# Products of taps ordered between the scatters of GpSimd in a fused convolution and mixture-of-experts kernel

## The chip, the cores and the metric

The kernel runs on one core of a Trainium2 chip. The metric is the device time of one execution in microseconds (us); the time of a kernel is the median of its runs. The engines are named as the profile names them: PE (TensorE), DVE (VectorE), ACT (ScalarE), POOL (GpSimd) and SP (SyncE, whose queue issues most of the transfers).

## The reference

A causal convolution of 7 taps, whose weights come per token and head from a softmax, is followed by a mixture of 8 experts, of which each token uses one.

```python
# x (8, 3584, 192) f32, weight_gen (8, 3584, 8, 7) f32
w = softmax(weight_gen, axis=-1)
out = np.einsum('bshk,bskhg->bshg', w, x_unf)      # x_unf: 7 tokens up to this one, 8 heads of 24
x = out.reshape(28672, 192)
logits = x @ w_gate                                 # 192 x 8
e_idx = np.argmax(logits, axis=1)
gate_w = softmax(logits)[e_idx]
eom = 1.0 / (1.0 + np.exp(-(x @ w_output_gate)))
for e in range(8):
    h = np.maximum(x[e_idx == e] @ w1[e], 0.0)      # 192 x 1024
    out[e_idx == e] = gate_w * eom[:, e] * (h @ w2[e])   # 1024 x 192
```

## The kernel before

The work has two halves that run side by side. The first half, called the front here, goes over 32 units of 896 tokens (u = 0 to 31, 7 tokens in each of 128 partitions). The second half goes over 81 tiles of up to 512 rows, all of one expert.

A unit passes these steps. Its x and its weights are loaded (`load_steps`). `softmax_steps` makes the weights. `tap_steps` makes one product x times weight for each tap: from unit 7 on, GpSimd makes taps 0 to 4 (tiles `gap`, each by two instructions, since the tokens before the unit lie in another buffer) and VectorE taps 5 and 6, and VectorE adds all seven in PSUM (`acc_steps`, rows `ps<-ps,gap`). For units 0 to 6 GpSimd makes four taps and TensorE adds them. There are five buffers for GpSimd's products from unit 7 on and one accumulator. `sum_steps` scales the sum and writes it in two halves of 16-bit numbers to the row buffer `rt`, of which there are three (RT); the rows are transposed by DMA (`gt`), TensorE multiplies them by the gate weights (rows `ps<-gm,gt`, the logits), and VectorE finds each token's expert. `weight_of_steps` computes the token's factor. `place_steps` computes each token's row in a buffer sorted by experts in DRAM, and then GpSimd sends the rows there by seven indirect DMAs, one for each token of a partition (`srtd<-rt,posi`). These are the first kind of scatter. `round_steps` finds out, after each unit, which tiles of 512 rows are certainly full; rows for which no full tile is certain stay back until the last unit.

A tile is loaded by the SP queue (`tile_load`: its rows transposed to `xT`, the expert's weights `wa` and `wb`), behind the scatters of its rows. TensorE multiplies it (`gemm_steps`): for a tile of 512 rows 40 matmuls with `wa`, whose results ScalarE and VectorE split into two halves (`hh`, `hl`), and for each group of 128 rows 24 matmuls with `wb`. ScalarE scales a group into `ys` (two buffers of four groups), and GpSimd sends it to the tokens' rows of the output by one indirect DMA (`out_dram<-ys,meta`). This is the second kind of scatter. The first six tiles (DEFER) are kept in DRAM and sent at the end (`out_dram<-yk,keep`).

The order of all engines' instructions is fixed when the program is made, by a list scheduler in the kernel itself. Every chain of steps is a generator that yields the engine of its next step. `Order.step` takes, again and again, the chain with the smallest key: the planned time at which its step could begin, which is the latest of the scheduler's clock, the chain's own time and the engine's time `t`; between equal times the chain of the smaller rank. Ranks, from first to last, are: split of h, output groups (RANK_Y), placing of rows (RANK_C), rounds, sums (RANK_B), taps (RANK_A), tiles. `Paced` wraps an engine and adds up planned costs to its `t`: a scatter 1.04, a product 0.06 + 0.00174 for each element. So on GpSimd an output group that is ready goes before rows of a unit, and these before a product. Each engine runs its queue in order, and semaphores hold an instruction until its operands are there. The lines of the profile are those of the wrappers: L151 is every compute instruction, L125 every transfer of the SP queue.

Of the kernel before, what the change touches and what calls it, by code (L numbers as in the profile page):

```python
# [67 lines left out]
class Chain:  # L68


    def __init__(self, gen, rank, t, engine):
        self.gen, self.rank, self.t, self.engine, self.gate = gen, rank, t, engine, None
        self.slack = EAGER[1] if len(rank) > 1 and rank[0] in EAGER[2] and rank[1] < EAGER[0] else SLACK
# [33 lines left out]
class Queue:  # L107
# [6 lines left out]
    @property  # L114
    def t(self):
        if self.host is not None:
            return self.host.t
        return max(self.moved, self.issued + self.lead)

    def __getattr__(self, name):  # L120
        f = getattr(self.engine, name)

        def call(*args, **kwargs):
            c, own, issue = self.order.cur, self.cost(name, args, kwargs), self.issue(name, args, kwargs)
            r = f(*args, **kwargs)  # L125
            if self.host is not None:
                self.issued = max(self.host.t, c.t)
                self.host.t = self.issued + issue
            self.issued = max(self.issued, self.order.now) + issue
            if own is not None:  # L130
                self.moved = max(self.moved, self.issued + 0.65) + own
                c.t = max(c.t, self.moved + 1.0)
            return r

        return call


class Paced:


    def __init__(self, order, engine, cost, before=0.0, after=None, lead=0.0, follows=True):
        self.order, self.engine, self.cost, self.t = order, engine, cost, 0.0
        self.before, self.after = before, LAT if after is None else after
        self.lead, self.follows = lead, follows

    def __getattr__(self, name):
        f = getattr(self.engine, name)

        def call(*args, **kwargs):
            c, own = self.order.cur, self.cost(name, args, kwargs)  # L150
            r = f(*args, **kwargs)  # L151
            if own is not None:
                self.t = max(self.t, (c.t if self.follows else self.order.now) + self.before) + own
                c.t = max(c.t, self.t + self.after)
            return r

        return call


def largest(args, kwargs):  # L160
# [50 lines left out]
def kernel(ctx: ExitStack, tc: tile.TileContext, x, wg, wgate, wogate, w1, w2, cst, out):  # L211
# [2 lines left out]
    V = Paced(od, nc.vector, vector_cost)  # L214
    S = Paced(od, nc.scalar, scalar_cost, after=LAT_S)
    G = Paced(od, nc.gpsimd, gpsimd_cost)
    T_ = Paced(od, nc.tensor, tensor_cost, after=0.0)
    SP = Queue(od, nc.sync, sync_cost, sync_issue, LEAD)
    TQ = SP if TURN_SP else Queue(od, nc.scalar, sync_cost, sync_issue, LEAD, S)
# [30 lines left out]
    def take(slots, engine):  # L250

        yield engine, lambda: slots
        got = slots.pop(0)
        od.cur.t = max(od.cur.t, got[0] if isinstance(got, tuple) else got)
        yield engine
        return got
# [27 lines left out]
    def has(u, *what):  # L284
        return lambda: all(k in U[u] for k in what)
# [33 lines left out]
    for i in range(RT):  # L319
        t = rp.tile([P, JS, WR], I32, name=f"rt_{i}")  # L320
# [68 lines left out]
    def gate_steps():  # L389
# [9 lines left out]
        S.activation(gsq, g32.rearrange("p a b -> p (a b)"), AF.Square, accum_out=gss)  # L399
        yield T_  # L400
        pg = ps[:, 2304:2320]
        T_.matmul(pg[:, 0:1], lhsT=ones32, rhs=gss, start=True, stop=True)
        yield V
# [27 lines left out]
    def split_steps(e, st1, st2):  # L431
# [4 lines left out]
        S.activation(sqd, st2, AF.Square, accum_out=ss[:, 1:2])  # L436
        yield from take(tr_free, T_)
        pg = ps[:, 1536:1538]
        T_.matmul(pg[:, 0:2], lhsT=ones32, rhs=ss, start=True, stop=True)
        yield V  # L440
# [101 lines left out]
    def tap_steps(eng, tag):  # L542

        for u in range(NU):
# [12 lines left out]
            while taps:  # L557
# [13 lines left out]
                if u < PE_U:  # L571
                    od.add(add_steps(u, t, tag, kind), (RANK_A, u, 3), T_)
                else:
# [53 lines left out]
    def add_steps(u, t, tag, kind):  # L627

        d = U[u]
        yield T_, lambda: "sum" in d or ("begun" not in d and (u == 0 or "sum" in U[u - 1]))  # L630
        if "begun" not in d:
            d["begun"] = 0
            _, at = yield from take(sum_free, T_)
            d["sum"], d["sum_at"] = ps[:, at : at + 1536], at
        n, flat = d["begun"], t.rearrange("p a b -> p (a b)")
        d["begun"] += 1
        for lo in (0, 512, 1024):
            hi = min(lo + 512, NV * GD)
            T_.matmul(d["sum"][:, lo:hi], lhsT=cf[:, 0:128], rhs=flat[:, lo:hi], start=(n == 0), stop=(n == K - 1 - PAIRS), skip_group_check=True)
        tap_free[tag].append((od.cur.t + LAT_P, kind))  # L640
        if n == K - 1 - PAIRS:
            d["total"] = d["sum"][:, 0 : NV * GD].rearrange("p (a b) -> p a b", b=GD)
            od.add(sum_steps(u), (RANK_B, u), S, T_.t + LAT_P)

    def sum_steps(u):
# [36 lines left out]
        else:  # L682
            od.cur.t += LAT_T
            for j0 in range(0, JS, 2):
# [38 lines left out]
        V.tensor_tensor_scan(out=p3e.rearrange("p e j -> p (e j)"), data0=segs, data1=ohe.rearrange("p e j -> p (e j)"), initial=0.0, op0=ALU.mult, op1=ALU.add)  # L723
        od.cur.t += LAT_R
        yield T_
# [75 lines left out]
    def place_steps(u):  # L801

        d = U[u]
        p3, rk = d["p3"], d["rk"]
        oh1 = d["oh"]
        yield V, has(u - 1, "ranked")
        ob = state["base"]
        ru = f_ru
        V.tensor_tensor(out=ru, in0=rk[:, 0:8], in1=ob, op=ALU.add)
        nb = cp.tile([P, NE], F32, tag="base", bufs=4, name=f"base{u + 1}")  # L810
        V.tensor_tensor(out=nb, in0=rk[:, 8:16], in1=ob, op=ALU.add)
        state["base"] = d["base"] = nb
        rk_free.append((od.cur.t, d["rk_at"]))
        d["ranked"] = True
        if u in plan:
            od.add(round_steps(u), (RANK_R, u), V)
        else:
            state["rounds"] += 1
        yield V
        pe = sp.tile([P, JS, 8], F32, tag="pe", name=f"pe{u}")  # L820
        V.tensor_tensor(out=pe, in0=p3, in1=ru.unsqueeze(1).broadcast_to([P, JS, 8]), op=ALU.add)
        yield V
        V.tensor_tensor(out=pe, in0=pe, in1=oh1, op=ALU.mult)
        done_with(u)
        yield V
        pos = sp.tile([P, JS], F32, tag="pos", name=f"pos{u}")
        V.tensor_reduce(out=pos, in_=pe, axis=AX, op=ALU.add)
        yield S
        posi = sp.tile([P, JS], I32, tag="posi", name=f"posi{u}")
        S.copy(posi, pos)  # L830
        d["placed"] = True
        yield G, has(u, "weighed")
        od.cur.t = max(od.cur.t, d["weighed_t"])
        for j in range(JS):
            yield G
            scattered(G.indirect_dma_start(
                out=srtd[:, :], out_offset=bass.IndirectOffsetOnAxis(ap=posi[:, j : j + 1], axis=0),
                in_=d["ri"][:, j, 0:W], in_offset=None, bounds_check=DUMMY - 1, oob_is_err=False))
        d["sent"] = True
        d["sent_t"] = od.cur.t + 2.5  # L840
        rt_free.append((d["sent_t"], d["ri"]))
# [94 lines left out]
    def tile_load(t, T, ti, i, writers, ka, kb):  # L936
# [11 lines left out]
        SP.dma_start(out=wb, in_=wd[bass.ds(e, 1), :, 2048:WW].rearrange("a p c -> p (a c)"))  # L948
        return dict(t=t, T=T, G=Gn, units=8 // (512 // T), wa=wa.bitcast(F16), wb=wb.bitcast(F16), inv=wb.bitcast(F32)[:, 1536:1537], meta=meta, xT=xT, ka=ka, kb=kb, hh=[], hl=[], hl_t=0.0)

# [22 lines left out]
    def gemm2_group(d, g, at):  # L973
# [6 lines left out]
        for f in range(8):  # L980
# [7 lines left out]
            T_.matmul(py, lhsT=hl, rhs=w2h, start=False, stop=(f == 7))  # L988
        if g == d["G"] - 1:
            wb_free.append((T_.t + WBX, d["kb"]))  # L990
        od.add(out_steps(d, g, py, at), (RANK_Y,), S, T_.t + LAT_P)

    def out_steps(d, g, py, at):
        if g == 0:
            S.activation(d["sc"][:, 0 : d["G"]], d["meta"].bitcast(F32)[:, 0 : d["G"], 0], AF.Copy, scale=d["inv"])
        S.activation(d["ys"][:, g, :], py, AF.Copy, scale=d["sc"][:, g : g + 1])
        y_free.append((od.cur.t, at))
        if d["t"] >= DEFER:
            yield G
            send(d["meta"][:, g, 1:2], d["ys"][:, g, :])  # L1000
        elif g == d["G"] - 1:
            t, n = d["t"], d["G"]
            keep = cp.tile([P, 4], I32, name=f"keep{t}")
            S.copy(keep[:, 0:n], d["meta"][:, 0:n, 1])
            yield SP
            yd = dp.tile([P, n, D], F32, name=f"yd{t}")
            SP.dma_start(out=yd, in_=d["ys"][:, 0:n, :])
            kept.append((keep, yd, n))
# [132 lines left out]
LAT_S = 0.13  # L1141
LAT_P = 0.3
LAT_T = 2.5
LAT_R = 1.0
SLACK = 0.1
EAGER = 0, 0.2, (2, 3, 4)
# [49 lines left out]
```

## Time and profile before

| what | us |
|---|---|
| median of three runs | 1300.61 |
| lowest and highest | 1295.26, 1304.66 |
| profiled execution | 1304.16 |
| its span, first to last instruction | 1302.4 |

The profile is of one execution. In its rows an instruction is named by its line, engine, operation and what it writes and reads (out<-in, the buffers' numbers left out); behind a bar stand the busy time, the mean length of one in ns, and the idle time of the engine just before the instructions, with what ended it. "issue" is idle time that ended for no reason that the profile shows.

### The profile page before, as it was taken

How to read it: one execution, taken by the hardware profiler on the slowest of the kernel's cores; microseconds unless marked ns; L12 is line 12 of the kernel's file. 1: busy time of each engine (PE TensorE's matmuls, PEld its weight loads, DVE VectorE, ACT ScalarE, POOL GpSimd, SP SyncE). 2: the span in 40 equal slices, each digit the busy share in tenths (PEclk: the TensorE clock that was granted, in tenths of full speed). 3: DMA queues.
4: the chain of work that ended last, by engine and by line, in shares of the span. 5: the costliest groups of instructions: out<-in, count | busy, mean ns of one | idle time of the engine just before them, and what ended most of it. 6: DMA issues, size and time to landing. Idle time of an engine off the chain costs nothing.

```text
span 1302.4 us, 28065 instructions
## 1 busy us (share of the span) xinstructions
PE 1147.5 (88%) x9958; PEld 834.1 (64%) x9958; DVE 1021.3 (78%) x2103; ACT 601.8 (46%) x1305; POOL 895.0 (69%) x776
## 2 busy tenths in 40 slices
PE   5886947898697988999997999989899999979998
PEld 2443426676464766676665766666566779878998
DVE  8898866999999999999999999999998633323332
ACT  3674642454353544554454554445454443434443
POOL 7689666667878887888898878998878534322222
PEclk9999878999898999999998999999999999999999
DMA  7777579889777977978797897768867899999994
GB/s 237 228 242 225 175 239 246 226 227 249 201 215 214 241 203 202 272 213 216 205 258 163 262 249 236 202 203 237 211 165 201 220 295 305 320 283 327 308 341 137
DMA packets 293853, 306.18 MB, mean 235 GB/s; under 512 B 232278, under 2 KB 253639, under 8 KB 283344
## 3 DMA queue, kind: packets, MB, share of 16 engines
q1 hardware_dynamic: 271728, 259.78, 70.7%
q0 software_dynamic: 21840, 44.30, 10.6%
q8 instruction: 78, 1.28, 0.4%
q14 instruction: 63, 0.52, 0.1%
q10 hardware_dynamic: 144, 0.31, 0.1%
HBM read 196.42 MB, written 62.01 MB: 198 GB/s over the span
## 4 chain that ended last, share of the span: by engine, by line
PE 38%; DVE 27%; POOL 10%; issue 10%; DMA 9%; ACT 3%; SPq 2%; POOLq 0%; DVEq 0%; ACTq 0%
PE ps L151 38%; DVE ps L151 13%; POOL gap L151 6%; DVE hl L151 4%; POOL srtd L151 3%; SPq L125 2%; DMA w<-in_wg_dram 2%; DVE vap L151 2%; DVE rt L151 2%; DMA wa<-wd 2%; POOL out_dram L151 2%; DMA srtd<-rt,posi 1%; ACT rt L151 1%; DVE w L151 1%; DVE vt L151 1%
## 5 line engine op out<-in xcount | busy, mean ns | idle before, releaser
L151 PE MATMUL ps<-xT,wa 128*128 128x512 f16 (+3 forms) x3240 | 561.1, 324 | 67.0 <-DVE hl L151 30.7
L151 PE MATMUL ps<-wb,hh 128*128 128x192 f16 x3696 | 479.6, 247 | 17.3 <-ACT ys L151 10.5
L151 DVE SCALAR_TENSOR_TENSOR hl<-ps,hh 128x512 f16<-128x512 f32 (+1 forms) x476 | 310.9, 666 | 191.4 <-ACT hh L151 188.3
L151 PE MATMUL ps<-wb,hl 128*128 128x192 f16 x1848 | 456.4, 247 | 0.0
L151 PEld LDWEIGHTS <-wa 128*128 128x128 f16 x3240 | 279.7, 99 | 259.3 <-issue 51.2
L151 POOL TENSOR_TENSOR gap<-x,w 128x960 f32<-128x960 f32 (+5 forms) x268 | 372.4, 1414 | 36.0 <-DVE w L151 13.3
L151 ACT ACTIVATE hh<-ps 128x512 f16<-128x512 f32 (+1 forms) x476 | 274.9, 583 | 229.3 <-PE ps L151 228.5
L151 PEld LDWEIGHTS <-hh 128*128 128x128 f16 x3696 | 337.7, 98 | 65.8 <-issue 25.1
L151 POOL DMA_INDIRECT out_dram<-ys,meta x216 | 214.3, 992 | 235.2 <-ACT ys L151 161.9
L151 POOL DMA_INDIRECT srtd<-rt,posi x224 | 230.0, 1027 | 90.7 <-issue 57.9
L151 ACT ACTIVATE ys<-ps,sc 128x192 f32<-128x192 f32 x231 | 97.1, 421 | 236.1 <-PE ps L151 153.5
L151 DVE TENSOR_TENSOR ps<-ps,gap 128x1344 f32<-128x1344 f32 x125 | 194.1, 1553 | 7.3 <-POOL gap L151 6.4
L151 PEld LDWEIGHTS <-hl 128*128 128x128 f16 x1848 | 181.7, 98 | 0.2
L151 POOL TENSOR_TENSOR gap<-halo,w 128x1152 f32<-128x1152 f32 (+4 forms) x38 | 62.4, 1642 | 18.9 <-issue 13.1
L151 PE MATMUL ps<-gap,cf 128*128 128x512 f32 x168 | 71.9, 566 | 2.7 <-POOL gap L151 2.7
L151 PE MATMUL ps<-vap,cf 128*128 128x512 f32 (+1 forms) x126 | 57.0, 596 | 13.1 <-DVE vap L151 13.1
L151 DVE SCALAR_TENSOR_TENSOR rt<-ps,sx,rt 128x448 f16<-128x448 f32 x64 | 57.6, 907 | 8.4 <-ACT rt L151 4.9
L151 PE MATMUL ps<-gm,gt 128*128 128x32 f16 x672 | 28.1, 177 | 41.0 <-ACT ys L151 12.3
L151 PEld LDWEIGHTS <-gt 128*128 128x128 f16 x672 | 25.2, 96 | 50.9 <-issue 35.7
L151 ACT ACTIVATE rt<-ps 128x1344 bf16<-128x1344 f32 x32 | 41.3, 1291 | 25.4 <-DVE ps L151 20.7
L151 PEld LDWEIGHTS ps<-gap,cf 128*128 128x128 f32 x168 | 31.3, 196 | 32.6 <-issue 26.8
L151 PEld LDWEIGHTS ps<-vap,cf 128*128 128x128 f32 x126 | 24.8, 208 | 36.8 <-issue 23.1
(115 smaller groups left out, 868.7 us busy)
## 6 DMA issues: line engine op xcount, KB each, us to landing
wa<-wd SPq DMA_DIRECT2D x81, 1024.0 KB
wb<-wd SPq DMA_DIRECT2D x81, 768.5 KB
x<-in_x_dram SPq DMA_DIRECT2D x32, 672.0 KB
w<-in_wg_dram SPq DMA_DIRECT2D x32, 196.0 KB
wd<-wpb SPq DMA_DIRECT2D x8, 768.5 KB
st<-in_w_dram SPq DMA_DIRECT2D x8, 768.0 KB
st<-in_w_dram SPq DMA_DIRECT2D x8, 512.0 KB
wd<-wpa SPq DMA_DIRECT2D x8, 512.0 KB
```

The costliest lines, as they stand in the source:

```text
L125: r = f(*args, **kwargs)
L151: r = f(*args, **kwargs)
```

## The change

A class `Apart` stands in for GpSimd where a chain yields it before a scatter. It shows the scheduler GpSimd's planned time plus 0.3 us (APART) when the last thing that GpSimd was given is a scatter, and the plain time otherwise. A product that is ready by then has the smaller key and is taken first, whatever its rank. The scatters themselves, their number and their operands stay as they are, and so do the products. It is used at three yields: two in `place_steps` and one in `out_steps`. The scatters of the six tiles kept back (`kept_steps`) use GpSimd itself.

```diff
@@ class Paced
-        self.lead, self.follows = lead, follows
+        self.lead, self.follows, self.last = lead, follows, None
...
             r = f(*args, **kwargs)
+            self.last = name
...
+class Apart:
+    def __init__(self, engine, name, cost):
+        self.engine, self.name, self.cost, self.lead = engine, name, cost, engine.lead
+
+    @property
+    def t(self):
+        return self.engine.t + (self.cost if self.engine.last == self.name else 0.0)
...
+    GS = Apart(G, "indirect_dma_start", APART)
@@ place_steps
-        yield G, has(u, "weighed")
+        yield GS, has(u, "weighed")
         od.cur.t = max(od.cur.t, d["weighed_t"])
         for j in range(JS):
-            yield G
+            yield GS
             scattered(G.indirect_dma_start(
@@ out_steps
         if d["t"] >= DEFER:
-            yield G
+            yield GS
             send(d["meta"][:, g, 1:2], d["ys"][:, g, :])
...
+APART = 0.3
```

## The prediction

> **What bounds the kernel now.** I read the page's busy line first, then a table of stretches, then the waits of the middle stretch, and last the chain of work that ended last.
>
> The first view is the page's head and its busy times.
>
> ```profile
> span 1302.4 us, 28065 instructions
> PE 1147.5 (88%) x9958; PEld 834.1 (64%) x9958; DVE 1021.3 (78%) x2103; ACT 601.8 (46%) x1305; POOL 895.0 (69%) x776
> ```
>
> TensorE is the busiest engine over the span, but the shares are averages over different stages. The table of stretches separates them: after the first column come the length, then the busy time of PE, PEld, DVE, ACT and POOL with instruction counts, the granted clock, the DMA share and GB/s.
>
> ```profile
> 0.00:300.00 300.00, 229.52 (x1380) 143.56 (x1381) 250.31 (x488) 150.48 (x297) 205.41 (x160) 0.92 0.77 227
> 300.00:1010.00 710.00, 637.99 (x5462) 449.18 (x5460) 670.02 (x1416) 337.59 (x767) 597.84 (x524) 0.98 0.81 219
> 1022.00:1302.00 280.00, 268.52 (x3006) 232.62 (x3003) 96.86 (x195) 109.04 (x232) 86.68 (x89) 0.99 0.90 289
> ```
>
> There are three stages. Up to 300 us the first units and the weights are prepared. From 300 to about 1020 the units of attention (the front) run beside the tiles of the experts: VectorE is busy 670.02 of 710 us (94%), TensorE 90%, GpSimd 84%. From 1022 on only expert tiles are left, and TensorE works 268.52 of 280 us (96%). The chain of work that ended last, in order of time, agrees; its columns are start, length and what:
>
> ```profile
> 1006.06 14.86 PE ps L151 x138
> 1021.42 133.63 PE ps L151 x1399
> 1155.67 6.42 DMA wa<-wd
> 1162.14 2.42 PE ps L151 x40
> 1165.21 5.24 DMA wa<-wd
> 1170.51 123.40 PE ps L151 x1448
> ```
>
> From 1021 on it is TensorE's own work but for two loads of weights. So two things set the time: when the front ends, and how much tile work is then still to do.
>
> GpSimd is fuller than its 84% says. The same stretch, grouped by form on GpSimd, gives its scatters; the columns behind the bar are busy time, mean ns of one, idle time before them and what ended it. Two groups' rows:
>
> ```profile
> L151 POOL DMA_INDIRECT srtd<-rt,posi x160 | 156.9, 980 | 50.7 <-issue 43.3 <-ACT rt L151 3.1 <-DVE w L151 1.6
> L151 POOL DMA_INDIRECT out_dram<-ys,meta x144 | 143.9, 1000 | 58.6 <-issue 17.2 <-ACT ys L151 12.2 <-ACT rt L151 5.4
> ```
>
> There are 160 + 144 = 304 scatters of about 1 us, and nearly all of GpSimd's idle time stands before them. The timeline of GpSimd shows how much of that is no wait at all:
>
> ```profile
> 452.81 2.72 POOL L151 TENSOR_TENSOR gap<-x,w 128x1152 f32<-128x1152 f32 x2
> 455.70 1.01 POOL L151 DMA_INDIRECT out_dram<-ys,meta  x1 [0.17 <-issue]
> 457.02 0.98 POOL L151 DMA_INDIRECT srtd<-rt,posi  x1 [0.30 <-issue]
> 458.30 0.98 POOL L151 DMA_INDIRECT out_dram<-ys,meta  x1 [0.30 <-ACT rt L151]
> 459.58 0.98 POOL L151 DMA_INDIRECT srtd<-rt,posi  x1 [0.30 <-issue]
> 460.58 2.71 POOL L151 TENSOR_TENSOR gap<-x,w 128x960 f32<-128x960 f32 x2
> ```
>
> A scatter behind a product costs 0.17 + 1.01 = 1.18 us, a scatter behind a scatter 0.30 + 0.98 = 1.28 us, and a product behind a scatter starts at once. GpSimd's idle time in the stretch is 710 − 597.84 = 112.2 us. At 0.17 to 0.30 us each, the 304 gaps are 52 to 91 us of it, so its real waits are 21 to 60 us: it is 92 to 97% taken.
>
> **The change part by part.** Its direct gain is the shorter gap. Counted in the order of GpSimd's queue, a scatter follows a scatter 231 times before the last product now, and 199 times in the changed kernel: 32 times less. Over the whole program the two counts are 330 and 324, since the scatters that are pushed back meet in the tail, where GpSimd has nothing else to do (86.68 busy of 280 us). The gain is 32 × (1.28 − 1.18) = 3.2 us of GpSimd. No product or scatter is added or removed.
>
> What else the rule does shows in GpSimd's order. srtd is the scatter of a unit's rows, out the scatter of a finished tile, gap a product; posi10 is unit 10, gap13_0 tap 0 of unit 13. Before, unit 10's last scatters and those of unit 11 come ahead of unit 13's products:
>
> ```order
> L151 DMA srtd_81<-rt_1_104,posi10_4367 230528x194 x4
> L151 DMA out_0_dram<-ys11_4443,meta11_3892 28672x192
> L151 DMA srtd_81<-rt_1_104,posi10_4367 230528x194 x2
> L151 DMA out_0_dram<-ys11_4443,meta11_3892 28672x192
> L151 DMA srtd_81<-rt_1_104,posi10_4367 230528x194
> L151 DMA out_0_dram<-ys11_4443,meta11_3892 28672x192
> L151 DMA srtd_81<-rt_2_106,posi11_4627 230528x194 x2
> L151 DMA out_0_dram<-ys11_4443,meta11_3892 28672x192
> L151 DMA srtd_81<-rt_2_106,posi11_4627 230528x194
> L151 TENSOR_TENSOR gap13_0_4755<-x12_3125,w13_3584 128x1152
> L151 TENSOR_TENSOR gap13_0_4755<-x13_3597,w13_3584 128x192
> ```
>
> In the changed kernel unit 10's last three scatters stand behind the last product of unit 14:
>
> ```order
> L151 DMA out_0_dram<-ys12_4679,meta12_4239 28672x192
> L151 TENSOR_TENSOR gap14_3_4893<-x13_3529,w14_4054 128x576
> L151 TENSOR_TENSOR gap14_3_4893<-x14_4064,w14_4054 128x768
> L151 DMA out_0_dram<-ys12_4679,meta12_4239 28672x192
> L151 TENSOR_TENSOR gap14_4_4920<-x13_3529,w14_4054 128x384
> L151 TENSOR_TENSOR gap14_4_4920<-x14_4064,w14_4054 128x960
> L151 DMA srtd_81<-rt_1_104,posi10_4111 230528x194 x3
> L151 DMA srtd_81<-rt_2_106,posi11_4765 230528x194 x7
> L151 DMA srtd_81<-rt_0_102,posi12_4934 230528x194 x2
> ```
>
> The products went ahead, the place between two of them goes to out (whose rank is higher than srtd's), and srtd collects in a long row. Up to unit 10's last scatter GpSimd now has 136 product instructions and 24 outs behind it, where it had 116 and 18: ten products of 2.72 us and six outs of 1.18 us, 34 us more. For the later units the same count gives between 6 us earlier and 36 us later, and for the last unit two outs fewer, 2 × 1.18 = 2.4 us earlier. So the rows of a unit come later in the middle, and level at the end. With the 3.2 us, the front's end can come 5.6 us earlier if GpSimd sets it, and 0 if it doesn't. VectorE is as full as GpSimd; I take −3 us, about the middle.
>
> Tiles are loaded after the rows they read, so TensorE's order follows. Here gt14 marks the last logit matmuls of unit 14, xT and wa are a tile's rows and weights. Before, it is tile 17 that comes next:
>
> ```order
> L151 MATMUL ps_85<-gm_228,gt14_5759 128x32
> L151 LDWEIGHTS gt14_5759
> L151 MATMUL ps_85<-gm_228,gt14_5759 128x32
> L151 LDWEIGHTS wa17_5668
> L151 MATMUL ps_85<-xT17_5666,wa17_5668 128x512
> ```
>
> Now it is tile 15:
>
> ```order
> L151 MATMUL ps_85<-gm_228,gt14_5331 128x32
> L151 LDWEIGHTS gt14_5331
> L151 MATMUL ps_85<-gm_228,gt14_5331 128x32
> L151 LDWEIGHTS wa15_5177
> L151 MATMUL ps_85<-xT15_5175,wa15_5177 128x512
> ```
>
> The tiles have fallen two behind. Counted in TensorE's order, 1904 tile matmuls precede unit 14's logits before, 1637 after: 267 fewer. At unit 31's logits, the last of the front, it is 5780 against 5712: 68 fewer. The tail's row prices a matmul at 268.52 us / 3006 = 89.3 ns, so 267 are 23.8 us and 68 are 6.1 us. The 68 have to be done after the front and lie bare: +6.1 us. The other 17.7 us have been made up by then, if TensorE can: between unit 14 and 1022 us, over 500 us, it would have to go from the middle's 90% to 94%, below the tail's 96%. I take 0 for it, with 17.7 us as the upper bound.
>
> ScalarE writes a tile's rows into ys, which out must have read before the buffer is written again; out comes between the products as promptly as before, so I put nothing there.
>
> **A lock in the middle.** Two tiny subtractions on VectorE are slow. The rows of VectorE's groups by form, over the whole span:
>
> ```profile
> L151 DVE TENSOR_TENSOR ps<-base,done 1x8 f32<-1x8 f32 x31 | 32.4, 1045 | 0.9
> L151 DVE TENSOR_TENSOR ps<-zt 1x9 f32<-1x9 f32 x31 | 24.5, 789 | 1.1
> L151 DVE TENSOR_TENSOR base<-ps,base 128x8 f32<-128x8 f32 x32 | 5.1, 158 | 0.2
> ```
>
> They take 1045 and 789 ns, where a subtraction of like size with one operand in PSUM takes 158. One case, on VectorE's and on GpSimd's timeline:
>
> ```profile
> 618.32 2.68 DVE L151 TENSOR_TENSOR ps<-zt 1x9 f32<-1x9 f32 x1
> ...
> 618.24 2.72 POOL L151 TENSOR_TENSOR gap<-x,w 128x384 f32<-128x384 f32 x2
> ```
>
> It ended when GpSimd's pair of products ended (620.96). In all this costs 31 × (0.887 + 0.631) = 47 us of VectorE. In the alternating stretches of the new order a product fills 2.72 of 2.72 + 1.18 us, 70%, and one that hits waits 1.36 us on average: 0.95 us each, against 0.76 now. If all 62 fell there, VectorE would lose 62 × 0.19 = 12 us; if all fell into the long rows of scatters, it would win the 47. I take 0, since as many products run in as long a front. The Trainium skill, "SBUF — State Buffer", section "SBUF: two separate sides", states that an instruction of VectorE with two SBUF inputs and one of GpSimd lock each other out of a shared port for the whole instruction. The trace agrees, and goes further: the lock lasted through two products in a row. By that rule the first of these ends, 12 us, is a rival below.
>
> **The sum.** −3 + 6.1 + 0 = +3 us. The profiled execution took 1304.16 us, 3.6 us above the median of the runs, 1300.61; against the median it makes 1304 us.
>
> **The rivals.** The first is faster. The waits of the middle stretch:
>
> ```profile
> POOL out_dram L151 <- ACT ys L151: 12.2, 9, 3.8
> DVE ps L151 <- POOL gap L151: 6.4, 9, 2.0
> POOL out_dram L151 <- ACT rt L151: 5.4, 6, 3.0
> POOL out_dram L151 <- ACT ez L151: 5.0, 6, 2.0
> ```
>
> GpSimd stood before outs that weren't ready, with products that could have run queued behind. If products first fills half of the middle of its 21 to 60 us of waits, 20 us, and the front ends so much earlier, the time is 1304 − 20 = 1284 us; with all 40 it would be 1264. For it speaks that GpSimd is nearly full; against it, that VectorE is as full and waited only 6.4 us for products. It decides from 16 us of filled waits on.
>
> The second is slower: rows that come late leave TensorE without a tile. The view of the DMA queue's own waits and TensorE's timeline:
>
> ```profile
> SPq L125 <- DMA srtd<-rt,posi: 152.7, 43, 10.9
> ...
> 406.33 3.77 PE L151 MATMUL ps<-xT,wa 128*128 128x512 f16 x10 [6.50 <-DMA wa<-wd]
> ```
>
> Already the queue that loads tiles waits 152.7 us for scattered rows, and at 406 TensorE stood 6.5 us for a tile. If none of the 17.7 us is made up and the front gains nothing, the time is 1300.6 + 23.8 = 1324 us. It gets worse if the units stall too, as there are three row buffers, and unit 13 needs the one that unit 10's last scatter frees. It decides once more than 10 us stay lost. Against it: the order's own count is nearly level at the end.
>
> The third is the lock: 1304 + 12 = 1316 us. That the change does nothing (330 against 324) is part of the forecast.
>
> **How the numbers follow.** Runs of before differ by 9 us, and 1% (13 us) is about what a measurement can tell. I give the forecast 0.38, the faster rival 0.27, the late rows 0.29, the lock 0.06. This makes faster 0.27, same 0.38, slower 0.35. The forecast's own range is 1291 to 1314. The range of 8 in 10 reaches into both rivals: down to 1278, a little below the first, and up to 1332, the second with a stalled unit of 8 us.
>
> **What would show it.** In the profile after: fewer gaps of 0.30 us on GpSimd in the middle; long rows of srtd; TensorE's waits on wa around 380 to 480 us; the start of the last unbroken tile stretch (1022 us now) a few us earlier, and the tail some 6 us longer. The forecast is wrong if that start moves by over 10 us, or if VectorE's wait for ACT or GpSimd changes the middle's 94%.

## The result, and the profile after

The changed kernel takes 1344.91 us, median of four runs (1336.26 to 1349.02), against 1301.93 us for the kernel before on the same chip (1295.26 to 1304.66): ratio 1.0315, 95% interval 1.0272 to 1.0358. The profiled execution took 1349.02 us, against 1304.16.

The head and the busy times of the page of the changed kernel:

```profile
span 1346.9 us, 28075 instructions
PE 1156.7 (86%) x9958; PEld 838.6 (62%) x9958; DVE 1003.5 (75%) x2103; ACT 606.9 (45%) x1305; POOL 895.6 (66%) x776
```

The span grew by 44.5 us. TensorE's busy time grew by 9.2 (1156.7 − 1147.5), its idle time by 35.3 (190.2 − 154.9). The 9958 matmuls are the same; the clock granted to TensorE is lower after, 0.951 against 0.968 over the span, and lowest where TensorE stands most (0.85 against 0.95 from 400 to 500 us, in the table below). The front's end is read from the tile view of the logits, which gives their count, their shortest, median and longest time in ns, and the start of the first and last. After, then before:

```profile
L151 PE MATMUL ps<-gm,gt x147: 176/176/209, 855.3 to 1059.3; 128*128 128x32 f16 x147
```

```profile
L151 PE MATMUL ps<-gm,gt x126: 176/176/179, 865.6 to 1021.6; 128*128 128x32 f16 x126
```

The last unit's logits come at 1059.3 us, 37.7 later. The table of stretches, cut there, first after and then before, shows where TensorE stood (columns as in the prediction):

```profile
0.00:400.00 400.00, 311.03 (x2112) 201.91 (x2113) 346.54 (x694) 197.66 (x406) 295.73 (x236) 0.93 0.77 223
400.00:500.00 100.00, 64.28 (x516) 42.77 (x515) 82.69 (x193) 36.41 (x83) 77.90 (x68) 0.85 0.74 199
500.00:1059.30 559.30, 505.63 (x4259) 355.52 (x4257) 474.65 (x1020) 259.94 (x577) 432.00 (x383) 0.96 0.79 207
1059.30:1346.90 287.60, 275.73 (x3083) 238.38 (x3078) 99.59 (x199) 112.87 (x239) 90.00 (x92) 1.00 0.89 283
```

```profile
0.00:400.00 400.00, 312.19 (x2074) 201.84 (x2074) 347.65 (x700) 195.53 (x405) 284.05 (x228) 0.93 0.77 222
400.00:500.00 100.00, 85.81 (x720) 59.80 (x721) 91.36 (x182) 44.22 (x101) 89.55 (x78) 0.95 0.83 233
500.00:1021.60 521.60, 480.60 (x4157) 339.64 (x4157) 485.42 (x1028) 252.94 (x568) 434.32 (x383) 0.99 0.81 217
1021.60:1302.40 280.80, 268.92 (x3014) 232.86 (x3010) 96.86 (x195) 109.15 (x232) 87.04 (x89) 0.99 0.90 288
```

Up to 400 us TensorE's busy times differ by 1.2 us. From 400 to 500 it stands 35.7 us instead of 14.2 (+21.5), from 500 to the front's end 53.7 instead of 41.0 (+12.7). After the front 3083 matmuls are left instead of 3014, and that stretch is 6.8 us longer. In the stretch of the prediction, 300 to 1010, VectorE falls from 94% to 86%, TensorE from 90% to 86%, GpSimd from 84% to 80%:

```profile
300.00:1010.00 710.00, 610.77 (x5141) 428.14 (x5141) 613.72 (x1330) 321.37 (x722) 565.33 (x494) 0.94 0.76 202
```

All three do less in the same time, so none of them became the bound. The waits of that stretch (engine, line, what it waited for: us, times, longest):

```profile
POOL out_dram L151 <- ACT ys L151: 53.9, 38, 4.6
PE ps L151 <- DMA wa<-wd: 40.7, 5, 20.6
POOL srtd L151 <- issue: 38.5, 139, 0.3
DVE hl L151 <- ACT hh L151: 25.1, 31, 2.7
POOL out_dram L151 <- issue: 13.8, 66, 0.3
```

TensorE's wait for weights before, in the same view:

```profile
PE ps L151 <- DMA wa<-wd: 11.3, 2, 6.5
```

and after the SP queue's own over the whole span:

```profile
SPq L125 <- DMA srtd<-rt,posi: 250.1, 42, 20.6
```

TensorE waits 40.7 us for tiles (before 11.3), the queue that loads them 250.1 us for scattered rows (before 152.7), GpSimd 53.9 us before outs that aren't written yet (before 12.2). The last is the wait that the faster rival wanted to fill; it grew. How much these waits grow depends on the chip. On one where the kernel before takes 1362 us, its twin with a third `ys` buffer (e7 below) has 6.5 us of the first, 141.6 of the second and 40.8 of the third, and the changed kernel (e5) 24.3, 168.2 and 58.9. The longest single hole, on GpSimd's timeline:

```profile
411.72 2.70 POOL L151 TENSOR_TENSOR gap<-x,w 128x576 f32<-128x576 f32 x2
414.60 1.01 POOL L151 DMA_INDIRECT out_dram<-ys,meta  x1 [0.17 <-issue]
415.64 2.71 POOL L151 TENSOR_TENSOR gap<-x,w 128x384 f32<-128x384 f32 x2
418.51 1.01 POOL L151 DMA_INDIRECT srtd<-rt,posi  x1 [0.17 <-issue]
419.83 0.98 POOL L151 DMA_INDIRECT srtd<-rt,posi  x1 [0.30 <-issue]
...
432.65 0.98 POOL L151 DMA_INDIRECT srtd<-rt,posi  x1 [0.30 <-issue]
```

the SP queue's:

```profile
402.29 0.36 SPq L125 DMA_DIRECT2D x<-in_x_dram  x1
426.35 0.41 SPq L125 DMA_DIRECT2D meta<-srtd  x1
426.90 1.51 SPq L125 DMA_TRANSPOSE xT<-srtd  x1
428.62 0.40 SPq L125 DMA_DIRECT2D wa<-wd  x1
```

and TensorE's:

```profile
435.05 11.31 PE L151 MATMUL ps<-xT,wa 128*128 128x512 f16 x40 [20.65 <-DMA wa<-wd]
```

This is the place of the prediction's second order listing. Unit 14's products alternate with outs from 400 to 418; only then come unit 10's last rows and those of units 11 and 12, in one row. The SP queue, whose next entry is a tile that reads such rows, issues nothing from 402.65 to 426.35. TensorE has no tile for 20.65 us.

Two times show that this goes on through the front. I worked them out from the engines' timelines as means over 14 units. The first is the time from the end of the instruction that finds a unit's rows (VectorE, `pos`) to the end of the unit's seventh scatter, over units 16 to 29. The second, called the slack here, is the time from there to the first write of the row buffer by the unit that takes it over, three units later, over the takers 17 to 30. Before they are 28.9 and 29.6 us, after 55.0 and 9.2. The rows leave 26 us later in the mean, and the slack for the next user of the buffer shrinks to a third. The distance from one unit's sum to the next, called the round here, grows from 31.7 to 35.0 us.

### The profile page after: what moved, and what is told of

Read it like the earlier page. It is cut to its first block, busy times and chain, and to the rows that moved or that the text cites. A ratio compares the mean times of both kernels' runs of the same rounds, so it can differ in the third digit from the quotient of the medians.

```text
span 1346.9 us, 28075 instructions
## 1 busy us (share of the span) xinstructions
PE 1156.7 (86%) x9958; PEld 838.6 (62%) x9958; DVE 1003.5 (75%) x2103; ACT 606.9 (45%) x1305; POOL 895.6 (66%) x776
## 4 chain that ended last, share of the span: by engine, by line
PE 35%; DMA 7%; DVE 4%; SPq 2%; issue 2%; POOL 2%; ACT 1%; POOLq 0%; DVEq 0%; ACTq 0%
PE ps L151 35%; DMA wa<-wd 3%; SPq L125 2%; DMA w<-in_wg_dram 2%; DVE ps L151 2%; DVE hl L151 1%; DMA srtd<-rt,posi 1%; DMA gt<-rt 1%; POOL gap L151 1%; POOL srtd L151 1%; POOL out_dram L151 1%; ACT ys L151 0%; ACT hh L151 0%; DVE vt L151 0%; DVE w L151 0%
## 5 line engine op out<-in xcount | busy, mean ns | idle before, releaser
L151 PE MATMUL ps<-xT,wa 128*128 128x512 f16 (+3 forms) x3240 | 562.6, 326 | 73.8 <-DMA wa<-wd 53.9
L151 PE MATMUL ps<-wb,hh 128*128 128x192 f16 x3696 | 483.6, 248 | 17.4 <-ACT ys L151 14.3
L151 DVE SCALAR_TENSOR_TENSOR hl<-ps,hh 128x512 f16<-128x512 f32 (+1 forms) x476 | 311.4, 667 | 205.4 <-ACT hh L151 204.6
L151 PE MATMUL ps<-wb,hl 128*128 128x192 f16 x1848 | 458.4, 248 | 1.6 <-DVE hl L151 1.3
L151 PEld LDWEIGHTS <-wa 128*128 128x128 f16 x3240 | 280.3, 99 | 269.6 <-DMA wa<-wd 66.4
L151 POOL DMA_INDIRECT out_dram<-ys,meta x216 | 214.0, 991 | 279.2 <-ACT ys L151 213.6
L151 POOL TENSOR_TENSOR gap<-x,w 128x960 f32<-128x960 f32 (+5 forms) x268 | 370.9, 1407 | 42.8 <-issue 16.3
L151 ACT ACTIVATE hh<-ps 128x512 f16<-128x512 f32 (+1 forms) x476 | 275.6, 583 | 255.8 <-PE ps L151 255.5
L151 PEld LDWEIGHTS <-hh 128*128 128x128 f16 x3696 | 339.2, 99 | 63.2 <-issue 24.3
L151 POOL DMA_INDIRECT srtd<-rt,posi x224 | 231.2, 1032 | 90.0 <-issue 57.3
L151 ACT ACTIVATE ys<-ps,sc 128x192 f32<-128x192 f32 x231 | 97.2, 421 | 256.6 <-PE ps L151 172.7
L151 DVE TENSOR_TENSOR ps<-ps,gap 128x1344 f32<-128x1344 f32 x125 | 194.4, 1555 | 2.2
L151 PEld LDWEIGHTS <-hl 128*128 128x128 f16 x1848 | 182.5, 99 | 2.6 <-DVE hl L151 2.2
L151 PE MATMUL ps<-gm,gt 128*128 128x32 f16 x672 | 30.3, 178 | 55.8 <-ACT ys L151 14.2
L151 PE MATMUL ps<-vap,cf 128*128 128x512 f32 (+1 forms) x126 | 60.6, 626 | 13.0 <-DVE vap L151 13.0
L151 POOL TENSOR_TENSOR gap<-halo,w 128x1152 f32<-128x1152 f32 (+4 forms) x38 | 63.6, 1675 | 10.5 <-DVE w L151 5.2
L151 DVE SCALAR_TENSOR_TENSOR rt<-ps,sx,rt 128x448 f16<-128x448 f32 x64 | 57.5, 908 | 17.3 <-ACT rt L151 13.1
L151 PE MATMUL ps<-gap,cf 128*128 128x512 f32 x168 | 68.5, 547 | 0.0
L151 PEld LDWEIGHTS <-gt 128*128 128x128 f16 x672 | 26.0, 97 | 67.7 <-issue 41.3
L151 DVE TENSOR_TENSOR vap<-x,w 128x960 f32<-128x960 f32 (+4 forms) x31 | 54.5, 1784 | 1.0 <-PE ps L151 0.9
L151 PEld LDWEIGHTS ps<-vap,cf 128*128 128x128 f32 x126 | 26.3, 221 | 38.7 <-issue 25.1
L151 PEld LDWEIGHTS ps<-gap,cf 128*128 128x128 f32 x168 | 30.4, 190 | 28.0 <-issue 26.1
```

## The experiments

All kernels of one comparison ran on one chip, beside the kernel before. Which chip matters: the kernel before took 1301.93 and 1301.51 us in two sessions and 1359 to 1364 us on four other chips. So only ratios within a chip are compared (the runs to e4 are from the first of the slower chips, those to e8 from the second, to e12 from the third, to e16 from the fourth, the last two from a chip as fast as the first); the expectations in us below were written for a kernel before of about 1301, unless they say otherwise. The change itself, repeated unaltered, gave 1.0129, 1.0182 and 1.0101 on three of the slower chips: the loss is there each time, but smaller. On the first of them, that of e1 to e4, it was not run.

What could make the 44 us: rows that leave late, so that tiles (and the load queue behind them) wait; the same late rows holding the row buffers, so that units wait; the outs that now stand between the products, with GpSimd waiting before them; the output buffers that those outs free; the one hole at 414 to 435; or the 0.3 us themselves, as a longer planned cost.

**One kind of scatter at a time.** The rule at the outs alone (the two yields of `place_steps` back to G), and at the rows alone (that of `out_steps` back to G):

```diff
-        yield GS, has(u, "weighed")
+        yield G, has(u, "weighed")
...
-            yield GS
+            yield G
```

> The 0.3 us is shown to the output scatters alone; a unit's row scatters go by GpSimd's plain time, as before. Theory R (row buffers: a unit's rows are sent so late that the sum of the unit three later waits for the row buffer, which lengthens the front by 38 us): the row scatters keep their old place in the order (unit by unit within 12 product instructions of before), so 1295 to 1315 us. Theory O (GpSimd stands before output scatters that are not ready, 54 us after against 12 before, since they were moved between the products): the outputs stay moved, so 1330 to 1350. Theory T (TensorE starves behind tile loads, 41 us on wa after against 11): 1300 to 1320, since tiles are at most 102 matmuls behind.

> The 0.3 us is shown to the row scatters alone. Theory R: the rows are as late as in the changed kernel (20 product instructions at unit 10, 10 to 18 from unit 15 to 28), so 1330 to 1355 us, with the sums of several units starting about 2 us after the last row scatter of the unit three before. Theory O: outputs go by their old time, so 1295 to 1315.

Outs alone: 1389.44 against 1361.28 us, 1.0198 (1.0139 to 1.0257). Rows alone: 1376.12, 1.0128 (1.006 to 1.0196). Each costs by itself. With outs alone the rows leave 26 us after their places are known, about as in the kernel before (28.9), and the hole is smaller; yet the ratio is not below the 1.010 to 1.018 that the whole change made on the other slower chips. It lies between what late rows alone would leave of the loss (1320 over 1301, 1.015, at most) and what the outs themselves would make (1330 over 1301, 1.022, at least), so neither theory is met. With rows alone they leave after 52.8 us, and the hole is as in the changed kernel; that ratio, too, lies between the two theories. From 400 to 500 us, outs alone, then rows alone:

```profile
400.00:500.00 100.00, 76.55 (x594) 52.67 (x593) 83.37 (x176) 38.16 (x85) 84.66 (x74) 0.89 0.73 190
```

```profile
400.00:500.00 100.00, 61.75 (x521) 42.02 (x521) 85.04 (x193) 36.39 (x84) 81.64 (x72) 0.85 0.77 198
```

**The buffers.** A fourth row buffer needs room, so the control has a smaller HB. In the first pair the order of all instructions stays, only the buffer that a unit uses changes:

```diff
-HB = 16
+HB = 14
...
-        _, ri = yield from take(rt_free, S)
+        yield from take(rt_free, S)
+        ri = rows[u % ROWS]
```

> The changed kernel with 14 instead of 16 h buffers, which frees room for the next kernel and is its control. The tiles are some 335 matmuls behind at the last unit's logits (30 us of TensorE) where the changed kernel was 68 behind, so all theories: 1340 to 1375 us.

> The same order of all engines as with 14 h buffers, but the units' rows go through four row buffers in turn instead of three. Theory R: the sums no longer wait for the row scatters of the unit three before, so the front's end (last unit's logits) comes 20 to 38 us earlier and the time falls by 15 to 38 us against the control. Theories O and T, and a front that is held by anything else in the order (outputs, tile loads, the SP queue): within 8 us of the control.

1404.5 and 1402.82 us, 1.0329 (1.0269 to 1.0389) and 1.0291 (1.0215 to 1.0366): no difference. But with the order kept, the next user's work still stands where it stood in the queues: units 13 and 24 began to write their rows 0.3 us after the last scatter of the unit three before, though they no longer needed its buffer (3.0 and 4.4 us after it in the control). So this pair shows that waiting for the buffer isn't the limit, not that the place in the order isn't. A third buffer for `ys` (bufs=3), in both kernels:

> The changed kernel as it is, as a control on this chip: all theories 1.025 to 1.037 times before, and a hole in TensorE's work between 400 and 500 us (60 to 70 us busy in that stretch).

> The same order of all engines, but three buffers for the tiles' outputs instead of two. Theory Y (output scatters that stand later on GpSimd hold the two output buffers, which the planner does not count, so that ScalarE and behind it TensorE stand): 0.8 to 3% below the control. Theory H (row scatters that come late leave TensorE without a tile between 400 and 500 us) and theory P (output scatters that are not ready hold up the products behind them): within 0.5% of the control.

> The kernel before with three output buffers, order unchanged. Theory Y: at most 0.5% faster than before, as ScalarE waited there for an output's transfer 11.5 us in all; theories H and P: within 0.5% of before.

The change again 1380.81, with the buffer 1380.92; the kernel before 1362.44, with the buffer 1365.07. The output buffers are not it.

**One hole, or all along?** The rule up to unit 14 and tile 13 only; from there on only; and everywhere but for the rows of units 9 to 12, which mends the hole. The edit of the first:

```diff
-        yield GS, has(u, "weighed")
+        E = GS if u < 15 else G
+        yield E, has(u, "weighed")
...
-            yield GS
+            yield E
...
-            yield GS
+            yield GS if d["t"] < 14 else G
```

> The 0.3 us is shown only before the row scatters of units 0 to 14 and the output scatters of tiles up to 13; what comes later goes by GpSimd's plain time. Unit 10's rows are as late as in the changed kernel. Theory H (one hole, never made up): 1.02 to 1.03 times before, nearly the whole loss. Theory P or a loss that is spread over the front: 1.00 to 1.02.

> The changed kernel as it is, the control for the three runs beside it: 1.010 to 1.036 times before, by the chip.

> The changed kernel, but the row scatters of units 9 to 12 alone go by GpSimd's plain time. In the order unit 10's rows then come 8 product instructions later than before, not 20, and at unit 14's logits the tiles are 68 matmuls behind, not 267. Theory H (unit 10's late rows leave TensorE without a tile for 20.65 us, and this is never made up): TensorE busy 75 us or more between 400 and 500 us and 0.8 to 1.6% below the control. Theory D (the loss is spread over the front, and whatever is late in one place is made up): within 0.5% of the control.

> The 0.3 us is shown only before the row scatters of units 15 and later and the outputs of tiles 14 and later; up to 400 us all is as before. Theory H: 0.998 to 1.008 times before, as no hole is there. Theory D: 1.010 to 1.025 times before.

The early half: 1391.44, 1.0182 (1.0125 to 1.024), beside 1.0129 for the whole change on that chip. On the next chip the whole change gave 1385.59, 1.0182 (1.0144 to 1.022), the late half 1397.98, 1.0248 (1.0213 to 1.0283), and the mended hole 1399.11, 1.0255 (1.0213 to 1.0298). Mended it was, as the stretch of that kernel shows (62.20 busy in the control):

```profile
400.00:500.00 100.00, 78.51 (x652) 54.48 (x651) 83.36 (x182) 41.07 (x95) 78.56 (x69) 0.93 0.76 191
```

Yet it is slower than the control, by 1.0%, which neither theory foresaw: its front ends at 1101.5 us, the control's at 1077.8. So the hole is one showing of the loss and not its cause, and each half of the program loses at least as much as the whole. The parts don't add up: an order that differs in one place differs in what is planned after it.

**Price or overtaking?** The rule does two things: it adds 0.3 us before a scatter that follows a scatter, and it lets a product of lower rank be taken in that time. The first can be had alone: the kernel before, whose scatter costs the planner 0.3 more behind a scatter, whatever is taken next (here also for the scatters of the six tiles kept back, which the change leaves alone).

```diff
+            if name == "indirect_dma_start" and self.last == name:
+                own += 0.3
+            self.last = name
```

With measured prices (e12) it is 0.1 there and 1.18 for a scatter; e14 puts the rule on top of e12; e15 is the changed kernel with APART = 0.1.

> The kernel before, in which the planner counts what the profile shows for a scatter, 1.18 us and 0.10 more behind another scatter, where it counted 1.04; no scatter is held back for a product, as the added time is not in what the planner compares. If the loss comes from the products being taken first, within 1% of before, and a little faster if plan and run fit better (0.985 to 1.005). If it comes from the longer planned times, 1.01 or more.

> The planner counts the same 0.3 us behind another scatter as in the changed kernel, but as a cost of the scatter; the comparison for the next step is the plain one, so no product overtakes a scatter that is ready. Theory V (overtaking: each overtaking puts a scatter off by a whole product of 2.72 us to save a gap of 0.10 us, and rows and outputs that come late lengthen the round of a unit): the loss goes, 0.98 to 1.003 times before. Theory C (the longer planned cost makes a looser order): like the changed kernel, 1.01 to 1.03.

> The true costs of the run before (1.18 us, 0.10 more behind another scatter), which were 0.983 times before, with the change's overtaking added. Theory V: the overtaking costs 1.3 to 4% here too, so 0.995 to 1.025 times before, and rows leave again some 50 us after their place is known instead of 32. Theory C and any loss that came from wrong planned costs: 0.975 to 0.99.

> The change with 0.1 us in place of 0.3, the gap that the profile shows. Products that are ready are still taken first, so theory V: most of the loss stays, 1.005 to 1.025 times before. Theory C: a third of the planned cost and of the loss, 1.003 to 1.010.

> The changed kernel as it is, the control on this chip: 1.010 to 1.036 times before.

| kernel | chip | us | ratio to before (95%) |
|---|---|---|---|
| measured prices, no overtaking (e12) | third slower | 1338.24 | 0.9826 (0.9791 to 0.9861) |
| 0.3 as a price, no overtaking (e13) | fourth slower | 1334.16 | 0.9815 (0.9758 to 0.9873) |
| measured prices and overtaking (e14) | fourth slower | 1389.27 | 1.0225 (1.0165 to 1.0285) |
| overtaking with 0.1 (e15) | fourth slower | 1398.32 | 1.0272 (1.0206 to 1.0338) |
| the changed kernel (e16) | fourth slower | 1372.24 | 1.0101 (1.0043 to 1.0159) |

This parts the change. The price without the overtaking makes the kernel 1.85% faster; with it, 1.0% slower: on the same chip the overtaking costs 1372.24 − 1334.16 = 38.1 us. A smaller APART doesn't make it smaller (e15). The stretch of the price alone (e13), then of the changed kernel on the same chip (e16):

```profile
300.00:1010.00 710.00, 632.16 (x5342) 443.79 (x5340) 631.11 (x1345) 322.25 (x738) 569.62 (x499) 0.97 0.77 211
```

```profile
300.00:1010.00 710.00, 606.79 (x5137) 426.33 (x5136) 611.13 (x1321) 316.80 (x715) 566.75 (x493) 0.95 0.74 201
```

GpSimd is as busy in both (569.62 and 566.75); TensorE does 205 matmuls more without overtaking (5342 − 5137). The rows leave 32.2 us after their places are known, against 57.8, the slack is 34.8 us against 8.8, and the round 33.8 us against 35.5. GpSimd's wait before outs that aren't written yet hardly differs, so it isn't what parts the two (first e13, whose L153 is the L151 of the others, then e16):

```profile
POOL out_dram L153 <- ACT ys L153: 45.5, 25, 2.9
```

```profile
POOL out_dram L151 <- ACT ys L151: 51.8, 28, 4.1
```

**Row buffers that the planner knows of.** Last, a fourth row buffer as RT = 4, so that the order uses it, with its control:

> The changed kernel with 14 h buffers again, the control of the run beside it: 1.02 to 1.04 times before.

> The changed kernel with 14 h buffers and four row buffers that the planner knows of, so that the order is made anew with them (the earlier run had four buffers in the order made for three). Theory R (the round of the three row buffers sets the pace of the units): the sums start earlier, the units' round falls from about 35 to 33 us or less, and the time is 1.5 to 4% below the control. Theory L (late rows cost wherever they are waited for; with more buffers the products overtake them further, up to 32 product instructions): within 1% of the control, with rows leaving later still, 60 to 90 us after their place is known.

1344.83 us, 1.0331 (1.0297 to 1.0366), and with four buffers 1350.31, 1.0381 (1.0348 to 1.0415). The front's last logits come at 1009.6 us instead of 1030.0: with overtaking and a fourth buffer in the plan the front is 20 us shorter. But the rows now leave 79.4 us after their places are known, the tiles stay behind, and 3492 matmuls are left after the front instead of 3347: what the front gains the tail pays. (The profiled execution with four buffers, 1342.99 us, is the fastest of its five.) The stretches behind the front, control and four buffers:

```profile
1030.00:1343.40 313.40, 307.63 (x3347) 261.68 (x3343) 110.31 (x215) 125.60 (x266) 99.27 (x102) 1.00 0.87 277
```

```profile
1009.60:1341.20 331.60, 325.87 (x3492) 274.56 (x3489) 116.90 (x224) 133.29 (x279) 102.02 (x105) 1.00 0.87 270
```

## Why the prediction was wrong

What the runs show together: taking products ahead of ready scatters costs the time, and the 0.3 us as a price doesn't (38.1 us between e16 and e13). It is paid for in two places, the front's end and the tile work left behind it, in shares that differ by chip. From the profiles, split at the last logits:

| kernel | chip | front's end | after it | matmuls left |
|---|---|---|---|---|
| before | first | 1021.6 | 280.8 | 3014 |
| changed | first | 1059.3 | 287.6 | 3083 |
| before, third `ys` buffer (e7) | second slower | 1075.8 | 286.3 | 3015 |
| changed (e5) | second slower | 1078.6 | 298.4 | 3082 |
| measured prices (e12) | third slower | 1061.8 | 275.0 | 2808 |
| changed (e9) | third slower | 1077.8 | 298.4 | 3080 |
| price alone (e13) | fourth slower | 1055.9 | 276.6 | 2913 |
| changed (e16) | fourth slower | 1071.1 | 298.9 | 3082 |

On the first chip the front pays 37.7 of 44.5 us. On the second slower one the kernel before (with the third `ys` buffer, which changed nothing) has lost that lead by itself, and what the change costs there (15 us of span) stands in the tail but for 3 us. Against a kernel with the better prices both places pay: 15 to 16 us in front, 22 to 23 behind.

**The direct gain** was right and of no account. In the traces a scatter follows a scatter 231 times before the last product, and 199 times after, as counted; the gaps are still 0.17 us behind a product and 0.30 behind a scatter. But each 0.1 us is saved by putting a product of 2.72 us ahead of a scatter that was ready.

**The front's end, "I take −3 us"**, is the step that failed: it came 37.7 us later, so the term was wrong by 41 us on the first chip. It said: 5.6 us earlier if GpSimd sets it, 0 if not. That bounds the end by GpSimd's amount of work, and leaves out that a unit can wait for rows that GpSimd still holds. The order's count had shown unit 10's rows 34 us late, and later ones 6 us early to 36 late; I set it aside because it was level at the last unit. At the prediction's own prices the counts make each of units 16 to 29 between 8 and 36 us late, 21 in the mean. Measured: rows 26 us later in the mean, the slack down from 29.6 to 9.2 us, the round 3.3 us longer. The round is longer on the slower chips too (34.1 to 35.5 us from e7 to e5, 33.8 to 35.5 from e13 to e16). That the late rows are what lengthens it, through the three row buffers, is argued: the four planned buffers brought the front's end 20 us earlier, but with e5 rows leave 28 us later than with e7 (57.8 against 29.7) and the front ends only 3 us later.

**"The other 17.7 us have been made up by then … I take 0."** The tiles were made up: the 267 matmuls behind became 69. The time wasn't: TensorE stood 21.5 us longer between 400 and 500 us and 12.7 after, while the front came later. I had asked only whether TensorE had room to catch up. That its standing made the front late is not shown: with the hole mended (e10) the front ended later still.

**The 68 matmuls at the front's end, +6.1 us**: 3083 − 3014 = 69, and the stretch is 6.8 us longer. The chain of the changed kernel still ends in TensorE's own work, but for three loads:

```profile
1036.20 22.43 PE ps L151 x184
1059.13 97.10 PE ps L151 x953
1156.74 7.63 DMA wa<-wd
1164.42 31.51 PE ps L151 x328
1201.71 6.81 DMA wa<-wd
1210.90 5.70 DMA wa<-wd
1216.65 121.76 PE ps L151 x1448
```

**The lock, "I take 0"**, went the other way than its rival. (The row of 158 ns that the prediction compares with is an addition, not a subtraction.) Over the span:

```profile
L151 DVE TENSOR_TENSOR ps<-base,done 1x8 f32<-1x8 f32 x31 | 17.5, 564 | 0.9
L151 DVE TENSOR_TENSOR ps<-zt 1x9 f32<-1x9 f32 x31 | 11.6, 373 | 1.1
```

VectorE won 56.9 − 29.1 = 27.8 us on them, and the kernel got slower all the same.

**The rivals.** What the second foresaw, late rows and TensorE without a tile, is what the trace shows; its price, 23.8 us and a little for a stalled unit, was about half of the 43 us, because it counted the tiles and gave the units 8 us only, and mending the largest hole gave nothing back. The faster rival fell with its premise: the waits before outs were not filled but grew from 12.2 to 53.9 us. Of the signs, the long rows of scatters, TensorE's wait around 414 to 435 us and the tail of some 6 us more came true; both that were to refute the forecast came too, the front's end moving by over 10 us and the middle's 94%, which became 86%.

**What stays open.** How overtaking becomes lost time. The lateness of the rows doesn't give it alone: the rule at the outs alone (e1) costs 2.0% though rows leave on time, and with 0.1 (e15) rows leave after 43.7 us with a slack of 16.4, less late than in the changed kernel on that chip (57.8 and 8.8), and it loses 2.7% against 1.0%. How far an order that is changed elsewhere moves the time is hardly measured: HB = 14 left the changed kernel's ratio at 1.0331, beside 1.0315, where the kernel before takes 1301 us (e17), but it is 1.0329 on a slower chip (e3), where the unaltered change made 1.010 to 1.018 on the other three. So part of each difference may be that. Against chance speaks that all ten orders with overtaking, two of them with HB = 14, are 1.0 to 3.8% slower than the kernel before, and the two with a higher price and no overtaking 1.7 to 1.9% faster. Why the price alone makes the kernel faster wasn't taken apart: its rows leave no earlier than those of the kernel before (32.2 against 28.9 us on the first chip and 29.7 with a third `ys` buffer on a slower one). And that rows leave late because places between products go to outs of higher rank is read from the order and the timelines; no run changed the ranks.

## What to carry to other kernels

An order that saves a little on each instruction by letting lower-ranked work pass must be priced by what the passed work holds: here 0.1 us a scatter against rows that leave 26 us later, with a buffer and a tile behind them. Try the cost of such a pair as a plain cost in the scheduler first (here 1.85% faster) and leave the choice to the ranks. And when a count of the order is level at the end, look at it in the middle: each unit's lateness, against the slack of what waits for it, could be counted before the run and warned of the loss, though it doesn't give its size.

## What the runs showed that was not expected

The same kernel, with the same instructions, takes 1301.5 to 1301.9 us in two sessions and 1359 to 1364 on four other chips, a difference of over 4%, more than the change makes on any of them. The slower profile has a lower granted clock (0.955 against 0.968) and more idle time for which nothing is recorded, for instance before weight loads from 500 to 1000 us (the kernel before, then its twin with a third `ys` buffer on a slower chip):

```profile
PEld L151 <- issue: 45.7, 65, 2.6
```

```profile
PEld L151 <- issue: 83.5, 101, 7.6
```

Its cause was not looked for. The two tiny subtractions on VectorE became faster (1045 to 564 ns, 789 to 373), though I had worked out that in alternating products and scatters they would hit a product more often. The changed kernel shows it on the slower chips too (e5: 465 and 378 ns; e7, the kernel before with a third `ys` buffer: 863 and 850). Alternation alone doesn't decide it: with measured prices and overtaking (e14), where a scatter follows a scatter 195 times as against the 199 of the changed kernel, they take 744 and 697 ns. The reason was not found.
